# Attention and a softplus feed-forward in one kernel: a new task order for the first chunk, new engines for some tasks, and the mask's load written later

## The chip, the core and the metric

The kernel runs on one core of a Trainium2 chip. The metric is the device time of one execution in microseconds (us). Before the change it is 913.67 us, the median of three runs (913.51 to 913.8).

## The reference

For 8 batches and 8 heads of 576 tokens and 64 channels, attention is computed with a mask: the first four heads see the last 32 keys, the other four see earlier keys at a distance that is a multiple of 32. All sums are in float32.

```
scores = scale * q @ k^T;  scores = where(mask, scores, -1e9)
attn = exp(scores - max);  attn = attn / (sum + 1e-9)
x = (attn @ v) as [4608 tokens, 512]
h = x @ w_in                      # [512, 2048]
g = max(h, 0) + log1p(exp(-|h|))  # softplus
out = g @ w_out                   # [2048, 512]
```

## The kernel before

The 4608 tokens go through the feed-forward in 9 chunks of 512. Each chunk has 16 blocks f of 128 hidden channels. A block is `hidden` (F: 12 matmuls of 128x512 into `ph`), softplus (A, Ae, Al on ScalarE; u, Gh, Gl, which split the result into a high and a low part), and `output` (O: 12 matmuls into four banks `py`). Each product is made of three: high by high, high by the weight's low part, low by high. So x and the weights are split too: x into x_h and x_l (tasks H and L), a weight block into `w_i` or `w_o`.

The weights come as raw 64-bit words. A block is loaded (wi, wo; 512 KB), then `a` on ScalarE, `B`, `d` and `c` on VectorE, then `h` (the high part, a cast) and `l` (the low part, a subtraction) on the engine that three lists name. All 32 blocks are prepared once, in the first chunk, and stay.

Attention works on pairs of heads: pair n has q, k and v loads (q, k, v), the layout of q for its two heads (D), the scores in a long and a short part (S0, S1, which end with a product that adds the mask), the maxima X, then for some parts a subtraction Y, one exponential E and sums Z, for others x and an exponential for each column; then r, R, M (normalisation), the transposes T with their copies C, the products with v (V), and H and L. Digits name the pair and then the part or half: X00 is the maximum of pair 0's long part, L21 the x_l of pair 2's second half. The first chunk of the feed-forward needs pairs 0 to 3. Its first block is cut in two: Fa0 (9 matmuls) needs pairs 0 to 2, F0 also pair 3.

The order of the first chunk is the text table `FIRST` (line 36), one word for each task. A loop near the end calls them in that order, and inside that call each engine's queue gets its instructions in the order written. The lists `ON_POOL`, `ON_VECTOR` and `ON_SCALAR` (from line 61) name tasks that are not on their usual engine. What comes after the first chunk is placed by the class `Plan`, which the change does not touch. Instructions ahead of the table, such as the mask's load and the identity, are not bound to the order in which they are written.

Loads are issued by SP in the table's order; the mask's load is issued by ScalarE. TensorE starts with eight products of no use to the result ("idle", task W).

Of the kernel before, what the change touches and what calls it, by code (L numbers as in the profile page):

```python
# [33 lines left out]


FIRST = """
W q0 k0 D01 D00 S00 S01 X00 Y00 q1 D10 X01 D11 x01 E00 Z00 k1 S11 X11 E01 r0 R0 M0 q2 D21 S10
T00 wi0 D20 Y11 X10 x10 ai0 Bi0 T01 di0 k2 E11 S21 Z11 S20 E10 ci0 v0 r1 C00 R1 M1 X21 x21 C01 V00
wo2 q3 ao2 Bo2 do2 co2 D30 hi0 D31 wi2 T02 C02 X20 Y20 k3 H00 L00 ai2 Bi2 E20 ho2 Z20 T10 wi1 di2
v1 E21 r2 T11 S31 V01 X31 S30 lo2 x31 R2 wo3 C10 T12 ci2 H01 L01 X30 Y30 ai1 C11 V10 C12 hi2 E31  # L40
wo0 M2 H10 L10 li2 E30 Z30 T20 C20 li0 r3 R3 ao3 Bi1 M3 T21 V11 C21 H11 L11 wi11 ai11 Bi11 di1 T22
T32 C32 di11 v2 wi3 V20 C22 H20 ci1 ci11 hi11 L20 T31 ai3 Bi3 v3 hi1 li1 C31 T30 C30 li11 wo1 wi4
V21 H21 L21 V31 di3 wo6 ao1 Bo1 ao0 ci3 V30 H31 L31 H30 L30 Fa0 hi3 li3 do1 Bo0 co1 do0 Bo3 q4 D4
wi12 co0 F0 A0 Ae0 ho1 k5 Al0 u0 lo1 Fa1 k4 S40 ai4 wi6 X40 Bi4 x40 ho0 lo0 wi5 Gh0 ai5 wi7 Bi5 F1
A1 Gl0 ai7 Ae1 Al1 E40 do3 co3 di4 u1 Gh1 ho3 lo3 F2 A2 Ae2 Bi7 ci4 di5 O0 q5 wi10 wo5 ao5 Al2 Gl1
wi8 S41 D5 X41 ci5 x41 E41 u2 Gh2 hi5 di7 li5 F3 hi4 A3 Bo5 do5 ci7 Ae3 Al3 r4 R4 li4 co5 O1 M4
S50 X50 x50 hi7 u3 wo12 v4 F5 F4 ho5 Gl2 lo5 Gh3 Gl3 P4 E50 S51 ai6 ai8 Bi8 di8 X51 O2 wo4 ao4 Bi6
wo7 x51 di6 ci6 hi6 A5 Ae5 Al5 u5 li7 Bo4 q6 A4 E51 r5 k6 D6 V40 ci8 do4 O3 H40 L40 S60 co4 R5
wi13 Ae4 ai10 Bi10 Al4 V41 H41 li6 wi9 M5 u4 Gh4 Gl4 X60 Gh5 ho4 x60 L41 P5 F7 F6 hi8 wo15 lo4 Gl5
li8 di10 v5 O4 k7 E60 ao6 Bo6 A7 ai13 S61 A6 Ae6 V50 O5 Al6 ci10 hi10 do6 co6 u6 wo11 wo8 q7 li10  # L50
F10 Ae7 Al7 X61 ho6 ai9 u7 x61 ao7 Bo7 do7 Bi13 di13 Bi9 Gh7 Gl7 ci13 H50 L50 wo14 lo6 di9 ci9 Gh6
Gl6 F8 D7 E61 r6 S70 co7 A10 Ae10 ao8 Al10 Bo8 do8 R6 hi9 A8 wi15 u10 V51 li9 X70 x70 O6 Ae8 Al8
co8 wo9 u8 M6 H51 L51 wi14 P6 ho8 lo8 ai12 Gh8 ho7 lo7 Gl8 F11 hi13 li13 Bi12 Gh10 Gl10 wo10 ao9
Bo9 F9 O7 E70 S71 ai15 Bi15 do9 X71 co9 v6 ao10 Bo10 A9 Ae9 Al9 x71 do10 V60 H60 L60 u9 ho9 A11 q8
lo9 Ae11 Al11 u11 O8 di15 ci15 Gh11 Gh9 Gl9 di12 V61 H61 ao11 Bo11 wo13 F13 hi15 li15 E71 r7 R7 O9
co10 ho10 A13 ci12 hi12 ao13 Ae13 Al13 k8 v7 Gl11 L61 lo10 do11 F15 ao12 O10 M7 co11 li12 ho11
lo11 u13 Gh13 P7 A15 Ae15 Gl13 ai14 Bi14 di14 ci14 F12 hi14 Al15 u15 O11 q9 A12 Ae12 Al12 u12 Bo12
D8 Gh12 V70 Qa0 li14 F14 do12 co12 ho12 Gl12 lo12 O12 Bo13 do13 A14 co13 ho13 lo13 H70 L70 V71
ao14 Bo14 do14 Ae14 co14 Al14 u14 ho14 lo14 O13 H71 L71 Q1 Gh14 v8 Gl14 O14 ao15 Bo15 do15 co15
Gh15 Gl15 ho15 lo15 QA1 Qu1 Qh1 Ql1 Q0 QA0 O15 y1 Ob15 y2 y3 Qu0 Qh0 y0 Ql0 k9  # L60
"""
# [904 lines left out]
```

## Time and profile before

| | before |
|---|---|
| median of three runs | 913.67 us |
| the profiled execution | 914.04 us |
| its span | 912.0 us |
| TensorE busy | 900.4 us, 99% |
| VectorE busy | 601.9 us, 66% |
| ScalarE busy | 446.3 us, 49% |
| GpSimd busy | 60.1 us, 7% |
| granted TensorE clock | 0.999 |

The span is the time from the first to the last instruction; the execution's time has 2.04 us around it. In the profile PE is TensorE, PEld its loading of weights, DVE VectorE, ACT ScalarE, POOL GpSimd, SP the engine that issues most loads. L328 is line 328: a helper's line can serve many tasks, L256 for instance every copy.

### The profile page before, as it was taken

How to read it: one execution, taken by the hardware profiler on the slowest of the kernel's cores; microseconds unless marked ns; L12 is line 12 of the kernel's file. 1: busy time of each engine (PE TensorE's matmuls, PEld its weight loads, DVE VectorE, ACT ScalarE, POOL GpSimd, SP SyncE). 2: the span in 40 equal slices, each digit the busy share in tenths (PEclk: the TensorE clock that was granted, in tenths of full speed). 3: DMA queues.
4: the chain of work that ended last, by engine and by line, in shares of the span. 5: the costliest groups of instructions: out<-in, count | busy, mean ns of one | idle time of the engine just before them, and what ended most of it. 6: DMA issues, size and time to landing. Idle time of an engine off the chain costs nothing.

```text
span 912.0 us, 14487 instructions
## 1 busy us (share of the span) xinstructions
PE 900.4 (99%) x5700; PEld 725.3 (80%) x5700; DVE 601.9 (66%) x1308; ACT 446.3 (49%) x795; POOL 60.1 (7%) x77
## 2 busy tenths in 40 slices
PE   8899999999999999999999999999999999999998
PEld 5677778888888888888888888888888888888886
DVE  7999997877767667766766676776776333333332
ACT  7898855445444444444544444445443333333332
POOL 4343540000000000000000000000000000000000
PEclk9999999999999999999999999999999999999999
DMA  9927212122211112111211121111200010001001
GB/s 339 349 102 246 81 30 73 43 57 67 70 39 43 43 44 89 32 42 43 89 44 43 43 78 27 42 43 43 89 18 17 1 46 1 1 1 47 0 1 47
DMA packets 49939, 58.27 MB, mean 64 GB/s; under 512 B 3152, under 2 KB 35024, under 8 KB 49872
## 3 DMA queue, kind: packets, MB, share of 16 engines
q1 hardware_dynamic: 49728, 57.16, 19.5%
q8 instruction: 45, 0.74, 0.3%
q10 hardware_dynamic: 144, 0.20, 0.1%
q14 instruction: 22, 0.18, 0.1%
HBM read 47.91 MB, written 9.44 MB: 63 GB/s over the span
## 4 chain that ended last, share of the span: by engine, by line
PE 90%; DVE 6%; ACT 1%; DMA 1%; issue 1%; POOL 0%; SPq 0%; ACTq 0%; DVEq 0%; POOLq 0%
PE py L647 42%; PE ph L607 41%; PE ps L328 3%; PE pv L484 2%; PE po L484 1%; DVE pt L432 1%; PE po L328 1%; DVE u L628 1%; DMA kT<-in_qk_dram 1%; DVE a_o L561 1%; DVE a_i L561 0%; ACT prob L374 0%; DMA raw_q<-in_qk_dram 0%; DVE a_o L578 0%; DVE a_i L578 0%
## 5 line engine op out<-in xcount | busy, mean ns | idle before, releaser
L647 PE MATMUL py<-w_o,gh 128*128 128x512 f32 x1152 | 365.7, 398 | 0.0
L607 PE MATMUL ph<-x_h,w_i 128*128 128x512 f32 x1152 | 358.8, 392 | 0.4 <-DVE u L628 0.4
L619 ACT ACTIVATE u<-ph 128x512 f32<-128x512 f32 x144 | 86.3, 600 | 409.0 <-PE ph L607 409.0
L647 PEld LDWEIGHTS py<-w_o,gh 128*128 128x128 f32 x1152 | 214.4, 188 | 51.8 <-POOL w_o L593 0.9
L607 PEld LDWEIGHTS ph<-x_h,w_i 128*128 128x128 f32 x1152 | 215.8, 188 | 48.9 <-DVE u L628 0.9
L647 PE MATMUL py<-w_o,gl 128*128 128x512 f32 x576 | 227.1, 394 | 0.0
L607 PE MATMUL ph<-x_l,w_i 128*128 128x512 f32 x576 | 225.9, 392 | 0.0
L628 DVE SCALAR_TENSOR_TENSOR u<-ph,u 128x512 f32<-128x512 f32 x144 | 98.9, 688 | 181.0 <-ACT u L624 179.2
L432 DVE STREAM_TRANSPOSE pt<-prob 32x192 f32<-32x192 f32 x448 | 137.1, 314 | 6.4
L647 PEld LDWEIGHTS py<-w_o,gl 128*128 128x128 f32 x576 | 108.6, 189 | 25.7
L607 PEld LDWEIGHTS ph<-x_l,w_i 128*128 128x128 f32 x576 | 108.1, 188 | 25.3
L640 DVE TENSOR_TENSOR gl<-u,gh 128x512 fp32r<-128x512 f32 x138 | 96.1, 697 | 11.2 <-ACT gh L256 0.3
L622 ACT ACTIVATE u<-u 128x512 f32<-128x512 f32 x144 | 91.0, 632 | 4.5
L624 ACT ACTIVATE u<-u 128x512 f32<-128x512 f32 x144 | 90.8, 631 | 4.4
L256 ACT COPY qT<-prob 64x576 f32<-64x576 f32 x56 | 70.6, 1260 | 0.3
L256 DVE CAST gh<-u 128x512 fp32r<-128x512 f32 x130 | 55.4, 426 | 10.6 <-PE py L647 0.5
L391 DVE TENSOR_TENSOR prob<-ps,mask_b 128x384 f32<-128x384 f32 x24 | 13.4, 558 | 53.6 <-PE ps L328 53.6
L328 PEld LDWEIGHTS ps<-kT,qT 128*64 128x64 f32 x720 | 23.6, 137 | 11.7 <-issue 8.8
L328 PE MATMUL ps<-kT,qT 128*64 128x64 f32 x720 | 28.0, 226 | 0.3 <-ACT qT L256 0.3
L484 PE MATMUL pv<-pt,v_in 128*64 128x96 f32 x396 | 22.2, 248 | 0.0
L422 DVE TENSOR_TENSOR prob<-prob,st 128x576 f32<-128x576 f32 x28 | 21.2, 758 | 0.9
L391 DVE TENSOR_TENSOR prob<-po,mask_b 128x192 f32<-128x192 f32 x24 | 8.6, 358 | 19.3 <-ACT x_h L522 19.3
(89 smaller groups left out, 516.7 us busy)
## 6 DMA issues: line engine op xcount, KB each, us to landing
out_dram<-o SPq DMA_DIRECT2D x36, 256.0 KB, 2.2
v_in<-in_v_dram SPq DMA_DIRECT2D x28, 320.0 KB, 3.7
ri<-in_moe_w_in_dram SPq DMA_DIRECT2D x16, 512.0 KB, 7.2
ro<-in_moe_w_out_dram SPq DMA_DIRECT2D x16, 512.0 KB, 7.7
prob<-in_qk_dram SPq DMA_DIRECT2D x28, 288.0 KB, 2.8
kT<-in_qk_dram SPq DMA_DIRECT2D x28, 288.0 KB, 3.0
v_in<-in_v_dram SPq DMA_DIRECT2D x28, 48.0 KB, 2.8
room<-in_v_dram SPq DMA_DIRECT2D x4, 320.0 KB, 7.2
```

Source lines behind the costliest of these rows:

```text
L256: (engine.copy if engine is nc.scalar else engine.tensor_copy)(dst, src)
L328: nc.tensor.matmul(ps[64 * place : 64 * place + 64, 64 * (x - lo) : 64 * (x - lo) + 64], lhsT=blocks_of(n)[:, c // 32].rearrange("p h l -> ...
L391: nc.vector.tensor_tensor(pv, sv, m, op=ALU.add)
L432: nc.vector.transpose(pt[32 * (i + c) : 32 * (i + c) + 32, h, a : a + hi - lo, 32 * i : 32 * i + 32,], src[:, lo:hi, 32 * c : 32 * c + 32],)
L484: nc.tensor.matmul(po[64 * h : 64 * h + 64, TILE * x : TILE * x + TILE], lhsT=vs[n][:, a, h, :], rhs=pt_of(n, a)[:, h, a % 2], start=True, ...
L607: nc.tensor.matmul(ph, lhsT=w32["i", f][:, half, cc * P : (cc + 1) * P], rhs=x_of(x, cc)[:, t0 : t0 + n], start=(i == 0), stop=(i == 3 * N ...
L619: nc.scalar.activation(us[c, f], phs[c, f], AF.Abs)
L622: nc.scalar.activation(u, u, AF.Exp, scale=-1.0)
L624: nc.scalar.activation(u, u, AF.Ln, bias=1.0)
L628: nc.vector.scalar_tensor_tensor(u, in0=phs.pop((c, f)), scalar=0.0, in1=u, op0=ALU.max, op1=ALU.add)
L640: engine.tensor_tensor(g, us.pop((c, f)), ghs[c, f].bitcast(F32), op=ALU.subtract)
L647: nc.tensor.matmul(py[t], lhsT=g[:, sl], rhs=w32["o", f][:, half], start=(f == 0 and n == 0), stop=(f == NFC - 1 and n == 2),)
```

## The change

The table has the same tasks in another order, the lists name other tasks, and the mask's load is written behind the copy of the identity.

```diff
 FIRST = """
-W q0 k0 D01 D00 S00 S01 X00 Y00 q1 D10 X01 D11 x01 E00 Z00 k1 S11 X11 E01 r0 R0 M0 q2 D21 S10
...
-V21 H21 L21 V31 di3 wo6 ao1 Bo1 ao0 ci3 V30 H31 L31 H30 L30 Fa0 hi3 li3 do1 Bo0 co1 do0 Bo3 q4 D4
...
+W wi2 ai2 Bi2 q0 D00 D01 k0 S01 q1 D11 q2 D20 di2 ci2 S00 D10 X01 k1 X00 Y00 E00 S11 X11 Y11 D21
...
+wo7 ao2 T31 q5 C30 v4 wi8 V21 C31 V31 H21 Bi1 D4 di1 ci1 L21 ho3 V30 H31 Fa0 Bo2 lo3 H30 do2 co2
...
 ON_POOL = """
-D10 D20 D30 ho2 r2 x31 hi11 hi3 x40 ho3 x41 hi5 x50 ho5 hi6 r5 x60 ho6 x61 x71 ho9 ho11 Gh13 hi14
-ho13 ho14
+D21 x01 D31 x10 hi2 x21 x31 ho3 hi1 hi7 ho0 x41 x50 ho5 ho4 hi9 x70 Gh11 hi14 ho14 ho15
...
 ON_VECTOR = """
-D00 M0 M1 lo2 C12 M3 li1 li3 lo0 Gl0 lo3 Gl1 li5 li4 li7 li6 li10 Gl7 lo6 Gl6 Gl10 Gl9 li15 Gl11
-lo10 M7 Gh12 li14 Gl12 Gl14 Gh15 Gl15
+D01 D10 M0 M2 M3 li5 li4 lo3 li1 lo2 Gh0 Gl0 lo0 Gh1 lo1 li10 Gl3 lo4 M5 Gl5 Gl6 li12 Gl9 li15
+lo10 Gl13 M7 Gh15 lo12 lo13 Gl14
...
 ON_SCALAR = """
-y1 y3
+y3
...
     mask_b = const.tile([P, 12 * 64], BF16, name="mask_b")
-    nc.scalar.dma_start(mask_b, masks)
...
     nc.scalar.copy(ident, ident_b)
+    nc.scalar.dma_start(mask_b, masks)
```

How the head of ScalarE's queue stands in the built program, before: raw_q are loaded q, early_h laid-out q.

```order
L161 ACT_TABLE_LOAD
L163 DMA mask_b<-in_masks_dram 128x768
L208 CAST room_113<-ident_b 128x128
L256 COPY early_h_91<-raw_q_153 64x32x18
L256 COPY early_h_93<-raw_q_181 64x32x18
L356 ACTIVATE prob_104<-prob_104 128x384
```

And now, where ri is a raw weight block (line numbers are one less, but for the mask's load):

```order
L160 ACT_TABLE_LOAD
L207 DMA mask_b<-in_masks_dram 128x768
L206 CAST room_112<-ident_b 128x128
L547 ACTIVATE a_i_155<-ri_153 128x512
L255 COPY early_h_90<-raw_q_158 64x18x32
L255 COPY early_h_92<-raw_q_170 64x32x18
L255 COPY early_h_94<-raw_q_173 64x18x32
```

The mask's load has kept its place; the step `a` of a weight block stands ahead of the first layout.

TensorE's queue right behind the idle products, before: py are the banks that hold the first scores, early_l holds k.

```order
L328 MATMUL py_106<-early_l_92,early_h_91 64x64 x12
L336 LDWEIGHTS ident_b
L336 MATMUL py_106<-mask_b,ident_b 128x384
L328 MATMUL py_107<-early_l_92,early_h_91 64x64 x6
L336 LDWEIGHTS ident_b
L336 MATMUL py_107<-mask_b,ident_b 128x192
```

And now:

```order
L327 MATMUL py_106<-early_l_91,early_h_90 64x64 x6
L335 LDWEIGHTS ident_b
L335 MATMUL py_106<-mask_b,ident_b 128x192
L327 MATMUL py_105<-early_l_91,early_h_90 64x64 x12
L335 LDWEIGHTS ident_b
L335 MATMUL py_105<-mask_b,ident_b 128x384
```

Pair 0's short part (6 products) now comes ahead of its long part (12).

VectorE's queue from its first copy of q, before: the reduction from a py into st is a maximum X.

```order
L256 COPY early_h_91<-raw_q_153 64x18x32
L364 TENSOR_REDUCE st_178<-py_106 128x6
L351 TENSOR_TENSOR prob_104<-py_106,st_178 128x384
L364 TENSOR_REDUCE st_178<-py_107 128x3
L368 TENSOR_SCALAR st_178<-st_178 128x3
L360 TENSOR_REDUCE st_178<-prob_104 128x6
```

And now:

```order
L551 TENSOR_SCALAR a_i_155<-a_i_155 128x512
L255 COPY early_h_90<-raw_q_158 64x32x18
L560 SCALAR_TENSOR_TENSOR a_i_155<-ri_153,a_i_155 128x512
L577 SCALAR_TENSOR_TENSOR a_i_155<-ri_153,a_i_155 128x512
L255 COPY early_h_92<-raw_q_170 64x18x32
L363 TENSOR_REDUCE st_192<-py_106 128x3
L363 TENSOR_REDUCE st_192<-py_105 128x6
L350 TENSOR_TENSOR prob_103<-py_105,st_192 128x384
```

Three steps of a weight block, a second copy of q and the short maximum have come ahead of X00 (the reduction of size 128x6).

## Rows read from the trace of the kernel before

**Rows 1.** Busy time by stretch: engines, granted clock, DMA share, GB/s.
```profile
0.00:7.54 7.54, 5.62 (x35) 2.65 (x37) 3.16 (x7) 3.93 (x4) 6.65 (x24) 1.00 0.76 245
7.54:35.38 27.84, 22.80 (x524) 16.65 (x524) 26.77 (x56) 22.14 (x65) 10.23 (x11) 1.00 1.01 355
35.38:148.00 112.62, 111.94 (x670) 87.29 (x668) 105.51 (x217) 89.07 (x203) 43.17 (x43) 1.00 0.39 134
```
**Rows 2.** TensorE's waits, whole span: us in total, times, longest.
```profile
PE ph L607 <- DVE u L628: 0.4, 1, 0.4
PE ps L328 <- ACT qT L256: 0.3, 1, 0.3
```
**Rows 3.** TensorE's timeline at Fa0: start, duration, [idle before].
```profile
34.73 0.72 PE L484 MATMUL pv<-early_l,room 128*64 128x96 f32 x12 [1.48 <-DVE x_l L520]
35.38 0.73 PE L607 MATMUL ph<-x_h,w_i 128*128 128x512 f32 x2
```
**Rows 4.** VectorE's timeline, 4 to 35 us.
```profile
4.26 0.73 DVE L256 COPY early_h<-raw_q 64x576 f32<-64x576 f32 x1 [0.33 <-DMA raw_q<-in_qk_dram]
7.54 0.56 DVE L364 TENSOR_REDUCE st<-py 128x6 f32<-128x384 f32 x1 [2.55 <-PE py L336]
...
14.50 1.49 DVE L578 SCALAR_TENSOR_TENSOR a_i<-ri,a_i 128x512 uint32<-128x512 uint32 x1
...
32.56 1.75 DVE L593 TENSOR_TENSOR w_i<-a_i,w_i 128x512 fp32r<-128x512 f32 x1
34.23 0.45 DVE L520 TENSOR_TENSOR x_l<-pv,x_h 128x288 fp32r<-128x288 f32 x1
```
**Rows 5.** TensorE's timeline at the first scores.
```profile
5.51 1.55 PE L328 MATMUL py<-early_l,early_h 128*64 128x64 f32 x24 [0.74 <-ACT early_h L256]
...
7.43 0.91 PE L328 MATMUL py<-early_l,early_h 128*64 128x64 f32 x12
...
8.54 0.91 PE L328 MATMUL py<-early_l,early_h 128*64 128x64 f32 x12
...
9.57 0.92 PE L328 MATMUL py<-early_l,early_h 128*64 128x64 f32 x24
```
**Rows 6.** ScalarE's timeline: the first layouts of q, and D4.
```profile
4.25 1.16 ACT L256 COPY early_h<-raw_q 64x576 f32<-64x576 f32 x1 [1.87 <-DMA raw_q<-in_qk_dram]
5.86 1.19 ACT L256 COPY early_h<-raw_q 64x576 f32<-64x576 f32 x1 [0.45 <-DMA raw_q<-in_qk_dram]
...
36.07 2.56 ACT L256 COPY qT<-prob 64x576 f32<-64x576 f32 x2
```
**Rows 7.** DMA issues, 0 to 60 us: count, KB each, us to landing.
```profile
prob<-in_qk_dram SPq DMA_DIRECT2D x2, 288.0 KB, 5.7
...
mask_b<-in_masks_dram ACTq DMA_DIRECT2D x1, 192.0 KB, 3.7
```
**Rows 8.** GpSimd's timeline.
```profile
8.70 1.25 POOL L256 COPY early_h<-raw_q 64x576 f32<-64x576 f32 x1 [1.15 <-DMA raw_q<-in_qk_dram]
...
32.43 1.32 POOL L593 TENSOR_TENSOR w_i<-a_i,w_i 128x512 fp32r<-128x512 f32 x1
```
**Rows 9.** VectorE by form, 7.5 to 34.2 us: busy us, mean ns | idle before.
```profile
L561 DVE SCALAR_TENSOR_TENSOR a_i<-ri,a_i 128x512 uint32<-128x512 uint32 x4 | 2.7, 686 | 0.0
...
L364 DVE TENSOR_REDUCE st<-py 128x3 f32<-128x192 f32 x4 | 1.4, 352 | 0.0
...
L368 DVE TENSOR_SCALAR st<-st 128x3 f32<-128x3 f32 x2 | 1.1, 556 | 0.1
L414 DVE TENSOR_SCALAR st<-st 128x9 f32<-128x9 f32 x3 | 0.9, 304 | 0.4 <-ACT prob L374 0.4
...
L578 DVE SCALAR_TENSOR_TENSOR a_o<-ro,a_o 128x512 uint32<-128x512 uint32 x1 | 0.7, 692 | 0.0
...
L256 DVE COPY early_h<-pt 128x384 f32<-128x384 f32 x1 | 0.5, 548 | 0.0
...
L368 DVE TENSOR_SCALAR st<-st 128x6 f32<-128x6 f32 x1 | 0.2, 171 | 0.0
```

More of the change, by code (lines that the diff above doesn't have):

```diff
@@ L36 @@
 FIRST = """
-W q0 k0 D01 D00 S00 S01 X00 Y00 q1 D10 X01 D11 x01 E00 Z00 k1 S11 X11 E01 r0 R0 M0 q2 D21 S10
[L38 to L41, printed above, removed]
@@ L42 @@
-T32 C32 di11 v2 wi3 V20 C22 H20 ci1 ci11 hi11 L20 T31 ai3 Bi3 v3 hi1 li1 C31 T30 C30 li11 wo1 wi4
-V21 H21 L21 V31 di3 wo6 ao1 Bo1 ao0 ci3 V30 H31 L31 H30 L30 Fa0 hi3 li3 do1 Bo0 co1 do0 Bo3 q4 D4
[L44 to L59, printed above, removed]
@@ L60 @@
-Gh15 Gl15 ho15 lo15 QA1 Qu1 Qh1 Ql1 Q0 QA0 O15 y1 Ob15 y2 y3 Qu0 Qh0 y0 Ql0 k9
+W wi2 ai2 Bi2 q0 D00 D01 k0 S01 q1 D11 q2 D20 di2 ci2 S00 D10 X01 k1 X00 Y00 E00 S11 X11 Y11 D21
+S10 x01 q3 E01 D31 k2 S20 Z00 E11 X10 r0 wi0 x10 ai0 S21 R0 M0 D30 Bi0 di0 wi3 ai3 X21 hi2 Z11 wi4
+v0 T00 Bi3 T01 C00 T02 ai4 C01 V00 ci0 k3 S31 di3 E10 S30 X20 li2 Y20 ci3 r1 x21 R1 H00 L00 X31
+C02 V01 M1 T11 E20 Z20 wi5 wo3 Bi4 ai5 Bi5 E21 di4 di5 H01 v3 r2 L01 x31 C11 hi0 T10 C10 wo2 R2 M2
+T12 ci5 hi3 E31 X30 Y30 li3 ci4 v1 V10 C12 H10 L10 li0 E30 Z30 T20 C20 hi4 wo0 wi1 T21 C21 wo12 r3
@@ new lines @@
+R3 M3 hi5 li5 k4 V11 H11 L11 v2 ao3 Bo3 do3 ai1 T22 q4 T32 C32 wi7 V20 C22 li4 co3 T30 H20 L20 wo1
+wo7 ao2 T31 q5 C30 v4 wi8 V21 C31 V31 H21 Bi1 D4 di1 ci1 L21 ho3 V30 H31 Fa0 Bo2 lo3 H30 do2 co2
+ao0 ho2 L31 hi1 ai7 L30 li1 lo2 F0 A0 wo4 Ae0 Bi7 S40 X40 Al0 x40 di7 ci7 hi7 Fa1 F1 u0 E40 Bo0
+S41 Gh0 ao1 Bo1 F4 wi11 wi13 A1 Ae1 Al1 wo5 ao5 do0 k6 co0 ho0 X41 D5 x41 u1 F2 wi6 Gl0 Bo5 lo0
+do5 O0 do1 A4 Gh1 co1 co5 Ae4 E41 r4 R4 wo13 Gl1 Al4 wi10 u4 ho1 lo1 ai10 Bi10 di10 k5 A2 Ae2 Al2
+M4 S50 X50 x50 li7 Gh4 Gl4 ho5 F3 wi9 ai9 u2 Gh2 E50 P4 Gl2 A3 O1 wo11 q6 ai6 Ae3 lo5 ci10 ao4 Bi9
@@ new lines @@
+F5 di9 Al3 u3 Bo4 O2 A5 hi10 Bi6 Ae5 li10 wo6 wo10 do4 co4 S51 Gh3 Gl3 Al5 V40 H40 L40 ao6 ho4 X51
+x51 wo8 D6 lo4 E51 Bo6 F7 ai8 A7 Ae7 Al7 di6 ci6 hi6 do6 r5 O3 Bi8 co6 di8 ci8 hi8 R5 S60 li6 u5
+Gh5 V41 H41 X60 ci9 ho6 x60 E60 M5 Gl5 u7 lo6 v5 O4 li8 ao7 Gh7 Gl7 F6 L41 A6 hi9 Ae6 k7 P5 Al6 u6
+F10 wo9 ao9 A10 li9 O5 Ae10 Al10 Bo9 do9 co9 ai13 Bi13 di13 S61 Gh6 wi14 X61 x61 ao8 q7 D7 Bo7 Gl6
+k8 do7 co7 ci13 E61 r6 V50 H50 F8 Bo8 do8 L50 hi13 li13 R6 u10 O6 A8 S70 co8 M6 Ae8 Al8 ho7 ho9
+ai11 lo7 X70 lo9 V51 H51 x70 u8 F9 P6 Gh8 wi12 ai12 v6 ho8 Gl8 E70 lo8 A9 Ae9 Al9 F13 ao11 O7 Gh10
@@ new lines @@
+S71 L51 V60 Bi12 Bi11 di12 ci12 di11 ci11 hi12 li12 O8 H60 ao10 L60 u9 Gl10 X71 wi15 ai15 hi11
+Bo10 do10 V61 Gh9 Gl9 Bi15 A13 H61 x71 Ae13 Al13 co10 di15 ci15 ho10 hi15 wo14 E71 u13 F12 A12
+Gh13 Ae12 li11 Al12 L61 O9 li15 F11 ao12 lo10 Bo11 O10 do11 Gl13 ai14 co11 u12 A11 Bi14 di14 r7 R7
+Ae11 ci14 Al11 M7 F15 Gh12 u11 ho11 v7 Qa0 lo11 ao14 Gh11 Gl11 A15 Ae15 O11 Al15 P7 u15 hi14 li14
+V70 Gl12 Bo12 do12 q8 Gh15 co12 H70 L70 ao13 Bo13 ho12 lo12 F14 A14 Ae14 do13 Bo14 do14 V71 O12
+Al14 u14 Gl15 H71 L71 Q1 wo15 ao15 co13 ho13 co14 lo13 O13 Gh14 Bo15 do15 D8 ho14 Gl14 lo14 co15
@@ L61 @@
+ho15 lo15 QA1 Qu1 Qh1 Ql1 Q0 QA0 Qu0 Qh0 Ql0 O14 Ob15 v8 y3 k9 O15 y2 y0 y1 q9
 """
 ON_POOL = """
-D10 D20 D30 ho2 r2 x31 hi11 hi3 x40 ho3 x41 hi5 x50 ho5 hi6 r5 x60 ho6 x61 x71 ho9 ho11 Gh13 hi14
-ho13 ho14
+D21 x01 D31 x10 hi2 x21 x31 ho3 hi1 hi7 ho0 x41 x50 ho5 ho4 hi9 x70 Gh11 hi14 ho14 ho15
 """.split()
 ON_VECTOR = """
-D00 M0 M1 lo2 C12 M3 li1 li3 lo0 Gl0 lo3 Gl1 li5 li4 li7 li6 li10 Gl7 lo6 Gl6 Gl10 Gl9 li15 Gl11
-lo10 M7 Gh12 li14 Gl12 Gl14 Gh15 Gl15
+D01 D10 M0 M2 M3 li5 li4 lo3 li1 lo2 Gh0 Gl0 lo0 Gh1 lo1 li10 Gl3 lo4 M5 Gl5 Gl6 li12 Gl9 li15
```

## The prediction

> **What bounds the kernel now.** I read the page's busy shares first, then the busy time by stretch, TensorE's waits, and last the timelines of single engines over the first 36 us. After the first 36 us TensorE never rests: from 35.38 to 148 us it is busy 111.94 of 112.62 us, and the waits that are left to it there are 0.4 us for a softplus result and 0.3 us for a q layout [rows 1, 2]. Its number of matmuls is the same in both orders. So the time is TensorE's work plus what it idles, and nearly all its idling lies ahead of the first feed-forward block (Fa0), which starts at 35.38 us [rows 3]. What the change can win or lose is mostly where Fa0 lands.
>
> What holds Fa0 back is VectorE. In the stretch from 7.54 to 35.38 us it is busy 26.77 of 27.84 us, TensorE only 22.80 and ScalarE 22.14 [rows 1]. The last wait before Fa0 is TensorE's, for the subtraction that makes x_l of pair 2's second half (L21): it runs at 34.23 us, releases the product V30 at 34.73, and Fa0 follows at 35.38, 1.15 us after L21 began [rows 3, 4]. VectorE itself gets going at 7.54 us, with the first row maxima (X00), which wait 2.55 us for TensorE's scores [rows 4]. From there to L21 it has 53 instructions and takes 34.23 - 7.54 = 26.7 us. Fa0 is therefore X00's start, plus that list, plus 1.15 us.
>
> **The change, part by part.**
>
> *The mask's load.* In the built order it does not move: on ScalarE it stands behind the table load in both kernels, ahead of the identity's copy, and waits for nothing. Cost 0. Had it moved behind that copy, it would have been issued before the first q is used at 4.25 us, and would be needed only by the first mask product, which ends the first scores [rows 5, 6]; it took 3.7 us to land [rows 7], so the price would be at most a few tenths of a microsecond.
>
> *The new head.* SP now sends a weight block (wi2, 512 KB) ahead of q0 (288 KB) and k0. Before, q0 is used at 4.25 us, the third load of that size (q1) at 5.86, the fifth (q2) at 8.70: 0.8 us for each load at first, 1.4 later [rows 6, 8]. 512 KB are 1.78 such loads, so q0 comes at 4.25 + 1.78 x 0.8 = 5.7, and k0 as load 3.78 at 6.5 to 7.0. ScalarE's half of the layout takes 1.16 and ends near 6.9; VectorE's half lies beside it. The first scores start at about 7.0 instead of 5.51 [rows 5, 6].
>
> The second step is their order: the short part S01 now goes ahead of S00, and X00 needs S00. Before, 2.03 us lie between S00's start and X00 (5.51 to 7.54), and S01 with its mask takes 1.11 (7.43 to 8.54). These are slow matmuls: the same 24 take 1.55 us at 5.51 and 0.92 at 9.57, a ratio of 0.6 [rows 4, 5]. At the slow pace X00 comes at 7.0 + 1.11 + 2.03 = 10.14; at the fast one the two parts take 0.6 x 3.14 = 1.9 and it comes at 8.9. The late end, if k0 takes a load's time more, is 11.0. Which pace holds then is not shown by the trace; I take the slow one, since before it still holds at 8.54 (twelve matmuls in 0.91). So X00 is 2.6 us late, with the ends +1.3 and +3.5.
>
> The granted clock reads 1.00, the 2.4 GHz level, in the stretch up to 7.54 us too, while the first scores' matmuls run slower than their twins at 9.57 [rows 1, 5]. The Trainium skill (TensorE: Matmul & The Clock Gate, Part 1: The HAM clock gate) says that the slow clock is the default and activity lifts it. The pause ahead of the first scores grows from 0.74 us to about 2.2, so by that rule S01 and S00 run slow, and the sum is the +2.0 below; at the fast pace it would be +0.7. No run here shows it yet.
>
> In the time until then VectorE prepares wi2 (L552, L561, L578, 0.69 us each at most), lays out two halves of q (0.73 each by the copy it had) and takes X01 (0.35): under 3.9 us that start near 5.5, when wi2 is there, and end before 10.1 [rows 4, 9]. That is real work out of the way, but of a later weight block, not of the list between X00 and L21.
>
> *The list from X00 to L21.* In the new order 51 instructions stand there. Against before it has one L561, one L578 and one L414 more (0.69, 0.69, 0.30), and one copy of transposed probabilities, one short maximum and three L368 fewer (0.55, 0.35, and 2 x 0.56 + 0.17) [rows 9]. By these means that is -0.5 us; with the undisturbed 0.17 for each L368 and L414 it is +0.1. I take 0, with those ends.
>
> *Collisions with GpSimd.* Some VectorE instructions took far longer than their twins while GpSimd was working: L578 1.49 and L593 1.75 instead of the 0.69 of an undisturbed L578 (GpSimd's own L593 ran from 32.43 to 33.75), and two L368 took 0.56 in the mean where a third took 0.17 [rows 4, 8, 9]. These cost 0.80 + 1.06 + 0.78 = 2.6 us. Before, six long GpSimd instructions (two q copies, one normalisation, three weight subtractions) stand in this stretch; the new lists put six of the same kinds there. Which VectorE instruction meets them is not shown. I take no difference; the ends are -2.6 (all gone) and +2.0 (two more).
>
> The Trainium skill (SBUF — State Buffer, SBUF: two separate sides) calls the port pair that VectorE shares with GpSimd "an exclusive lock, not a bandwidth split", held for a whole instruction. The rows agree in the one case: VectorE's L593 ended 0.56 after GpSimd's. By that rule each of the six could hold VectorE up for its whole 1.3 us, 7.8 in all, so the late end of the sum would be +5.2 over before rather than +2.0.
>
> *Everything behind Fa0.* The order of blocks and weights to the end of the first chunk is new too, with three GpSimd instructions fewer and three g_low more on GpSimd. TensorE's work there is the same, and VectorE's, by the counts of the two built orders, by less than 1 us. It costs only where TensorE waits. Before it waits 0.7 us there [rows 2]; reaching every block later, it gives its suppliers more time, so I take 0.6 off. The ends are -0.7 and +1.5. The copies of the results (one moved from ScalarE to VectorE) lie beside TensorE's next block.
>
> *The sum.* 2.6 + 0 + 0 - 0.6 = +2.0 us. The profiled execution took 914.04 us (span 912.0 and 2.04 around it), 0.37 over the median of the runs; 914.04 + 2.0 = 916.0, or 915.7 on the scale of the median 913.67.
>
> **The rivals.**
>
> *The lateness is absorbed.* The fast pace, k0 early and no wait behind Fa0: +1.3 - 0.7 = +0.6, or 914.3. For it: where the pace changes is seen in one execution only. Against it: it was still slow at 8.54 before, with a shorter pause ahead.
>
> *GpSimd's new places cost VectorE nothing* (not slower). VectorE reads scores from PSUM while GpSimd copies; the collisions go: 2.6 - 2.6 - 0.6 = -0.6 on the median, 913.1; at the fast pace too -1.9, or 911.8. It decides from 2.0 us of collisions gone, where the sum is zero. For it: the lists are spread anew, and one small maximum and its scaling leave VectorE. Against it: as many long GpSimd instructions stand in the same stretch, beside the same weight work.
>
> *ScalarE is late with the last x* (slower still). D4, two copies of 2.56 us together [rows 6], stands in the new table ahead of H31 and H30; before it came behind them. Both are needed for F0, which stands right behind Fa0's nine matmuls. If q4, which took 5.7 us to land [rows 7], lands only when L21 runs, F0 waits up to 2.6: +4.6, or 918.3. Against it: ScalarE idles 5.7 of 27.84 us there [rows 1] and should reach D4 early.
>
> **How the numbers follow.** About 0.2% (1.83 us: 911.84 to 915.50) is what a measurement of this kernel can tell from no change. The forecast has 0.45, its own range 914.6 to 916.8, and some 0.11 of it lie inside the bound. The absorbed lateness has 0.25, nearly all of it within. GpSimd has 0.15, of which 0.09 are faster. The late x has 0.15, nearly all slower. Together: faster 0.10, within 0.42, slower 0.48. The range leaves out the ends where several terms fall on one side: 912.4 to 918.6.
>
> **What would show it.** Right: wi2 lands first, S01 starts near 7.0 and X00 near 10.1; L21 and Fa0 2 to 3 us later than 34.23 and 35.38; the stretch from X00 to L21 again close to 26.7; the mask's issue still at 0.75; TensorE without idling from Fa0 to 148 us. Wrong: X00 before 8.9 (the head), a stretch X00 to L21 under 25 (collisions or list), or TensorE idling over 1.5 us between Fa0 and the end of the first chunk (the blocks' new order). If Fa0 is not later than 35.38 and the time still grows, the whole reading of the head is wrong.

## The result, and the profile after

The changed kernel takes 916.40 us (median of 6 runs, 915.91 to 917.76); the kernel before took 913.64 beside it (6 runs, 912.82 to 914.08). The ratio is 1.0033, 95% interval 1.0020 to 1.0046: slower by 2.8 us, where 2.0 were forecast. The profiled execution took 916.61 us, its span is 914.6.

TensorE's timeline of the kernel after (start, duration, what ran, idle time before it) answers to [rows 3, 5]:

```profile
7.20 0.57 PE L327 MATMUL py<-early_l,early_h 128*64 128x64 f32 x12 [2.43 <-ACT early_h L255]
...
7.88 0.99 PE L327 MATMUL py<-early_l,early_h 128*64 128x64 f32 x24
8.81 0.50 PE L335 MATMUL py<-mask_b,ident_b 128*128 128x384 bf16 x1
10.01 0.91 PE L327 MATMUL py<-early_l,early_h 128*64 128x64 f32 x12 [0.70 <-ACT early_h L255]
...
11.12 1.55 PE L327 MATMUL py<-early_l,early_h 128*64 128x64 f32 x24
...
38.31 0.72 PE L606 MATMUL ph<-x_h,w_i 128*128 128x512 f32 x2
```

The short part S01 starts at 7.20 us and S00 at 7.88, both at the fast pace; the mask product that ends S00 runs from 8.81 to 9.31, and from there on the products are slow (S10: 1.55 for 24). Fa0 starts at 38.31, 2.93 us later than before [rows 3].

VectorE's timeline of the kernel after, its starts and its long steps up to L21, answers to [rows 4]:

```profile
5.83 0.51 DVE L551 TENSOR_SCALAR a_i<-a_i 128x512 uint32<-128x512 uint32 x1 [1.91 <-ACT a_i L547]
...
8.39 1.52 DVE L255 COPY early_h<-raw_q 64x576 f32<-64x576 f32 x1
9.84 0.80 DVE L363 TENSOR_REDUCE st<-py 128x3 f32<-128x192 f32 x2
...
13.15 0.56 DVE L363 TENSOR_REDUCE st<-py 128x6 f32<-128x384 f32 x1 [0.70 <-PE py L335]
...
14.06 1.22 DVE L421 TENSOR_TENSOR prob<-prob,st 128x576 f32<-128x576 f32 x1
15.21 1.49 DVE L551 TENSOR_SCALAR a_i<-a_i 128x512 uint32<-128x512 uint32 x1
...
25.94 1.76 DVE L577 SCALAR_TENSOR_TENSOR a_i<-ri,a_i 128x512 uint32<-128x512 uint32 x1
...
37.16 0.45 DVE L519 TENSOR_TENSOR x_l<-pv,x_h 128x288 fp32r<-128x288 f32 x1
```

The row at 9.84 is two maxima, X01 and then X00, which therefore starts near 10.08 (9.84 + 0.80, less the 0.56 that X00 took before). VectorE did not wait there: the scores were ready at 9.31, and it was still in its own queue. From X00 to L21 are 37.16 - 10.08 = 27.1 us.

The long GpSimd steps of the kernel after answer to [rows 8]:

```profile
8.14 1.36 POOL L255 COPY early_h<-raw_q 64x576 f32<-64x576 f32 x1 [2.09 <-DMA raw_q<-in_qk_dram]
...
14.76 1.66 POOL L592 TENSOR_TENSOR w_i<-a_i,w_i 128x512 fp32r<-128x512 f32 x1
...
25.61 3.21 POOL L592 TENSOR_TENSOR w_i<-a_i,w_i 128x512 fp32r<-128x512 f32 x2 [2.10 <-DMA ro<-in_moe_w_out_dram]
```

Each lies beside a long row of VectorE's. The busy time by stretch of the kernel after (length, busy time of PE, PEld, DVE, ACT and POOL with counts, granted clock, DMA share, GB/s) answers to [rows 1]:

```profile
7.20:10.14 2.94, 2.24 (x40) 1.59 (x42) 2.91 (x5) 2.51 (x2) 1.36 (x1) 0.74 1.04 400
10.14:37.16 27.02, 22.56 (x498) 16.56 (x498) 25.63 (x53) 21.09 (x65) 9.77 (x11) 0.90 0.86 300
37.16:38.31 1.15, 0.65 (x12) 0.53 (x13) 1.15 (x4) 1.14 (x2) 0.61 (x1) 1.00 0.93 336
38.31:148.00 109.69, 109.02 (x659) 85.65 (x658) 103.36 (x215) 88.10 (x201) 42.40 (x38) 1.00 0.38 131
```

L21 to Fa0 is 1.15 again. Behind Fa0 TensorE lacks 0.67 us up to 148 us, against 0.68 before [rows 1], and TensorE's waits (us in total, times, longest) name 0.6 of it, for k of pair 5 [rows 2]:

```profile
PE pv L483 <- DVE x_l L519: 4.5, 5, 2.1
...
PE ps L327 <- DMA kT<-in_qk_dram: 0.6, 1, 0.6
```

The span grew by 2.6 and Fa0 came 2.93 later: what is to be explained is the head. The 0.3 us that came back behind it are no more than profiles differ there (next section).

### The profile page after: what moved, and what is told of

Its sections match the earlier page's. It is cut to its first block, busy times and chain, and to the rows that moved or that the text cites. A ratio compares the mean times of both kernels' runs of the same rounds, so it can differ in the third digit from the quotient of the medians.

```text
span 914.6 us, 14491 instructions
## 1 busy us (share of the span) xinstructions
PE 900.8 (98%) x5700; PEld 726.0 (79%) x5700; DVE 603.9 (66%) x1310; ACT 447.8 (49%) x796; POOL 59.3 (6%) x74
## 4 chain that ended last, share of the span: by engine, by line
PE 94%; DVE 3%; DMA 1%; ACT 1%; issue 0%; SPq 0%; DVEq 0%; ACTq 0%
PE py L646 44%; PE ph L606 43%; PE ps L327 3%; PE pv L483 2%; PE po L483 1%; PE po L327 1%; DMA kT<-in_qk_dram 1%; DMA ri<-in_moe_w_in_dram 0%; DVE a_i L577 0%; DVE a_i L560 0%; DVE a_i L551 0%; ACT prob L373 0%; DVE st L363 0%; DVE early_h L255 0%; DVE x_l L519 0%
## 5 line engine op out<-in xcount | busy, mean ns | idle before, releaser
L606 PEld LDWEIGHTS ph<-x_l,w_i 128*128 128x128 f32 x576 | 108.1, 188 | 25.5 <-DVE x_l L519 0.3
```

The costliest lines, as they stand in the source:

```text
L606: nc.tensor.matmul(ph, lhsT=w32["i", f][:, half, cc * P : (cc + 1) * P], rhs=x_of(x, cc)[:, t0 : t0 + n], start=(i == 0), stop=(i == 3 * N ...
```

## The experiments

All were timed beside the kernel before, whose medians in the four sessions lay between 913.31 and 913.41. In the diffs only the words of the table that move are shown, for e2, e7 and e8 at their new place only. "After" is the changed kernel. Its own interval is 1.8 to 4.2 us above the kernel before, and it was timed in another session, so differences of under about 1 us between the medians of after and of its versions are not clear of noise; the profiles, one execution each, show where the time lies. In every profile but four, the stretch from Fa0 to the end of the span is 876.0 to 877.0 us, so Fa0's start is the first number to look at; the four are e1, e7, e9 and e12.

**e2: the load of wi2 alone.**

```diff
-W q0 k0 D01 D00
+W wi2 q0 k0 D01 D00
```

> The kernel before with one word moved: the load of wi2 is issued first, ahead of q0 and k0; all computing on wi2 stays where it was. Theory (the load's price goes through): the first layout of q starts 1.2 to 1.5 us later than 4.25, S00 at 6.7 to 7.0, X00 at 8.7 to 9.1, and Fa0 and the time are 1.2 to 1.5 us later than before. Rival (a late start is absorbed between X00 and Fa0, since later loads and transposes then wait less): X00 is late by the same, Fa0 by less than 0.7, time under +0.6 us.

914.66 us, ratio 1.0014 (1.0006 to 1.0023). ScalarE's first layout, and VectorE's X00 and L21:

```profile
5.87 1.16 ACT L256 COPY early_h<-raw_q 64x576 f32<-64x576 f32 x1 [3.49 <-DMA raw_q<-in_qk_dram]
```

```profile
9.15 0.56 DVE L364 TENSOR_REDUCE st<-py 128x6 f32<-128x384 f32 x1 [2.58 <-PE py L336]
...
35.20 0.44 DVE L520 TENSOR_TENSOR x_l<-pv,x_h 128x288 fp32r<-128x288 f32 x1
```

q came 1.62 us later than in [rows 6], X00 1.61, L21 0.97. The list was 0.6 shorter because the collisions fell differently: one small step of VectorE took 0.17 instead of 0.94. The median rose by 1.25. So the load's price goes through in the time, as the prediction had it, though Fa0 came only 0.96 later, less than the theory's 1.2 to 1.5.

**e8: the load and the steps of wi2 in front, scores in the old order.**

```diff
-W q0 k0 D01 D00 S00
+W wi2 ai2 Bi2 q0 k0 D01 D00 di2 ci2 S00
```

> The kernel before with the load of wi2 in front as in e2 and also its steps ai2, Bi2, di2, ci2, as in after; the scores keep the old order, the long part first. Theory (VectorE's list from X00 to Fa0 sets the time): X00 starts at 9.1 as in e2, but three steps of 0.42 to 0.69, 1.7 us together, have gone from the list behind it, so Fa0 comes 0.6 to 1.0 us earlier than before's 35.38 and the time is 912.4 to 912.9. Rival (the prediction's reading: a late start goes through and the steps put ahead of X00 are no gain): the time is that of e2, 1.0 to 1.5 us above before. Rival (collisions fall differently): any value between, with a VectorE step of 1.3 us or more that was short in before.

914.14 us, ratio 1.0012 (1.0003 to 1.0021). X00 started at 9.22 and L21 at 34.68: the stretch is 25.5 us against 26.05 in e2. So the steps that run while the scores are awaited do come off the list, but of their 1.7 us only about 0.5 arrived at L21 and in the medians (a difference that the intervals of e2 and e8 do not separate); 0.76 went into new waits of VectorE for ScalarE (0.53 for an x_h, 0.23 for an exponential), the rest I cannot name. The result lies between the first theory and the first rival.

**e3: the long part first.**

```diff
-k0 S01 q1 D11 q2 D20 di2 ci2 S00 D10
+k0 S00 q1 D11 q2 D20 di2 ci2 S01 D10
```

> The kernel after with S00 and S01 exchanged, so that the long part is multiplied first. The prediction's step (the short part ahead of the long one is what X00 waits for): X00 starts 0.6 to 1.1 us earlier than 10.1 and the time falls by 0.6 to 1.1 us from after. Rival (X00 waits for VectorE's own queue: the steps of wi2, two layouts and X01 stand ahead of it, and the scores have been ready since 9.3 us): X00 and Fa0 stay within 0.2 us of after, the time too.

916.70 us (915.49 to 918.49), ratio 1.0039 (1.0027 to 1.0052): no gain over after. In this profile VectorE's D10 began at 8.39, just ahead of GpSimd's D21 at 8.46; this time D10 took 0.69 and GpSimd's copy 1.67. The pair of maxima started at 9.28, waiting only 0.20 for TensorE, and X00 came at 9.5 and L21 0.66 earlier than in after, but the time did not follow. D10 was 0.83 shorter, which by itself is more than the 0.5 at X00, so the prediction's 1.1 us for putting the short part ahead are not there.

**e4: no collision ahead of X00.**

```diff
-D20 di2 ci2 S00 D10 X01 k1 X00 Y00 E00 S11 X11 Y11 D21
+D20 D21 di2 ci2 S00 D10 X01 k1 X00 Y00 E00 S11 X11 Y11
 ON_POOL = """
-D21 x01 D31
+x01 D31
```

> The kernel after with the layout of q2's second half (D21) on ScalarE, right behind D20, instead of on GpSimd. In after GpSimd's copy ran from 8.14 to 9.50 and VectorE's layout D10 took 1.52 us beside it instead of 0.65. Theory (VectorE's queue ahead of X00, stretched by that collision, sets X00): D10 takes about 0.7, X00 starts 0.6 to 0.9 us earlier than 10.1, Fa0 follows by as much, time 0.5 to 0.9 us below after. Rival (X00 waits for the scores or the time is lost elsewhere): D10 is short but Fa0 and the time stay within 0.2 us of after; or ScalarE's extra 1.2 us delays the first exponential and S20, and the time is 0.3 to 1.0 us above after.

916.02 us (915.36 to 917.69), ratio 1.0034 (1.0022 to 1.0045). D10 took 0.68, and X00 still started at 10.0, now waiting for the scores. TensorE and VectorE in this profile:

```profile
7.98 1.55 PE L327 MATMUL py<-early_l,early_h 128*64 128x64 f32 x24
...
55.00 0.92 PE L327 MATMUL ps<-kT,qT 128*64 128x64 f32 x24 [1.60 <-DMA kT<-in_qk_dram]
```

```profile
10.01 0.56 DVE L363 TENSOR_REDUCE st<-py 128x6 f32<-128x384 f32 x1 [0.67 <-PE py L335]
```

Here the slow products began 0.8 us earlier than in the profile of after, in S00. So two limits stand within 0.2 us of each other at X00, VectorE's queue and slow scores, and taking one away leaves the other. The list was a microsecond shorter (26.04), mostly because after's step of 1.76 us took 0.69 here and the wait of 0.70 was gone, so Fa0 came at 37.20. S50 then waited 1.6 us for k5, which landed at 55.0 as in after: of 1.1 us at Fa0, 0.5 reached the span and 0.4 the median.

**e7: k5 ahead of k6, on top of e4.**

```diff
-F1 u0 E40 Bo0 S41 Gh0 ao1 Bo1 F4 wi11 wi13
+F1 u0 E40 Bo0 S41 Gh0 ao1 Bo1 F4 k5 wi11 wi13
```

> e4 with one word moved: the load k5 stands ahead of wi11 and so ahead of k6, whose issue waits until S41 has read its buffer. In e4 Fa0 came 1.1 us earlier than in after, but the time fell by only 0.4: S50 waited 1.6 us (in after 0.6) for k5, which landed at 55.0 us in both. Theory (that load gives the gain back): the wait is gone, Fa0 as in e4 near 37.2, and the time is 1.3 to 1.7 us below e4, 914.3 to 914.8. Rival (the loads are one full queue, and another one is late instead, a weight block for F2 or F3): the wait for k5 goes and another of 0.8 us or more comes; time less than 0.6 below e4.

917.94 us (916.80 to 919.51), ratio 1.0049 (1.0036 to 1.0062): by the medians slower than e4 by 1.9, with intervals that overlap. The wait for k5 went, and TensorE's waits show others in its place:

```profile
PE ps L327 <- ACT prob L373: 1.2, 2, 0.7
...
PE py L646 <- DVE w_o L592: 0.6, 1, 0.6
```

These are 1.2 us in S41 and S50 and 0.6 for a weight's low part. This execution also had slow scores from the start (S01 0.91, X00 at 10.28, Fa0 at 38.29), which is no effect of k5. From Fa0 to the end of the span it is 877.7 us against 876.9 in e4, so 0.8 lies behind Fa0, where k5 can be the cause. That the loads are one full queue fits; the rest of the 1.9 stays open.

**e5: the pause ahead of the scores filled.**

```diff
-    first["W"] = lambda: dummies(8)
+    first["W"] = lambda: dummies(12)
```

> The kernel after with 12 idle products ahead of the first scores instead of 8, to fill the pause of 2.4 us (4.77 to 7.20) in which TensorE waits for q. In after the granted clock falls to 0.50 at 8.7 us, behind that pause, and comes back at 15.3; S10 takes 1.55 instead of 0.92 and VectorE waits 0.70 for it. Theory (the fall follows the pause): the granted clock stays 1.00 from 7 to 16 us, the scores run in 0.92 and 0.57, and the time falls by 0.3 to 1.2 us. Rival (the fall has nothing to do with the pause): a stretch at 0.50 is there as in after, and the time stays within 0.2 us. Third (it costs): the added products are still running when q is laid out, S01 starts after 7.4 and the time grows by 0.2 us or more.

915.31 us (9 runs, 914.64 to 916.51), ratio 1.0024 (1.0015 to 1.0034); 7 of the 9 runs lie below the lowest of after's. Busy time by stretch, after (first fence) and e5 (second):

```profile
7.20:8.50 1.30, 1.30 (x33) 1.14 (x35) 1.27 (x3) 1.16 (x1) 0.36 (x1) 1.00 1.03 402
8.50:15.50 7.00, 6.30 (x88) 4.63 (x82) 6.16 (x12) 5.28 (x13) 3.98 (x6) 0.51 1.09 387
```

```profile
7.20:10.14 2.94, 2.60 (x55) 2.00 (x57) 2.87 (x6) 2.31 (x2) 1.46 (x2) 1.00 1.04 400
10.14:16.00 5.86, 5.52 (x142) 4.04 (x141) 5.72 (x12) 5.78 (x17) 3.91 (x6) 1.00 1.10 378
28.00:34.00 6.00, 5.95 (x119) 4.25 (x122) 5.83 (x13) 5.21 (x12) 0.61 (x1) 0.72 0.55 178
```

In after TensorE has the 1.2 GHz level from 8.6 to 15.4 us; in e5 it keeps 2.4 GHz past 16, all the first scores are fast, VectorE waits for none of them, and Fa0 comes at 36.60. A fall came here too, but at 29.6 to 33 us. Not all of the gain is the clock's. VectorE's D10, GpSimd's D21 and TensorE's Fa0 in e5:

```profile
8.26 0.68 DVE L255 COPY early_h<-raw_q 64x576 f32<-64x576 f32 x1
```

```profile
8.59 1.40 POOL L255 COPY early_h<-raw_q 64x576 f32<-64x576 f32 x1 [2.25 <-DMA raw_q<-in_qk_dram]
```

```profile
36.60 0.72 PE L606 MATMUL ph<-x_h,w_i 128*128 128x512 f32 x2
```

D10 was not stretched, since q2 landed later than in after and GpSimd began behind it. That is 0.84 of the 1.71 us by which Fa0 came earlier, and e3 had it without any change to the pause; the wait for S10 that went is 0.70. The median fell by 1.1, or by 0.8 when each version is taken against the kernel before of its own session. How much of that is the pause, and how much q2's landing, is not separated.

**e10: hi2 and li2 earlier on GpSimd.**

```diff
-S10 x01 q3 E01 D31 k2 ... X21 hi2 Z11 ... X20 li2 Y20
+S10 x01 q3 E01 D31 hi2 li2 k2 ... X21 Z11 ... X20 Y20
 ON_POOL = """
-D21 x01 D31 x10 hi2
+D21 x01 D31 hi2
```

> The kernel after with hi2 and li2 directly behind D31 in GpSimd's queue, ahead of x10, and x10 on VectorE (0.17 us). In after li2 ran on GpSimd from 14.76 to 16.42, and beside it VectorE's normalisation M0 took 1.22 us instead of 0.76 and the step Bi0 1.49 instead of 0.42: 1.5 us together. Theory (the collisions are part of the list that sets Fa0): both are short, the stretch from X00 to L21 shrinks from 27.0 to 25.6 to 26.2, and the time falls by 0.7 to 1.4 us from after, 915.0 to 915.7. Rival (the collision only moves to another VectorE step): another step grows by 0.7 us or more, and the time stays within 0.4 us of after. Rival (VectorE's list has slack elsewhere): short steps, but new waits of VectorE of 0.7 us or more ahead of L21.

916.35 us (915.90 to 916.60), ratio 1.0035 (1.0022 to 1.0047). The two steps were as short as expected, and Fa0 came 1.26 us earlier than in after. VectorE, then TensorE:

```profile
14.23 0.76 DVE L421 TENSOR_TENSOR prob<-prob,st 128x576 f32<-128x576 f32 x1
14.91 0.42 DVE L551 TENSOR_SCALAR a_i<-a_i 128x512 uint32<-128x512 uint32 x1
```

```profile
37.05 0.73 PE L606 MATMUL ph<-x_h,w_i 128*128 128x512 f32 x2
...
44.47 0.57 PE L327 MATMUL ps<-kT,qT 128*64 128x64 f32 x12 [0.47 <-ACT prob L373]
...
54.42 0.92 PE L327 MATMUL ps<-kT,qT 128*64 128x64 f32 x24 [0.86 <-DMA kT<-in_qk_dram]
```

The span fell by 0.6 and the median by 0.05. No theory named this: the collision is real, the list sets Fa0, and half of the gain ends in waits behind Fa0 (0.47 and 0.86, where after had 0.6 in all). Whether the other half is there in the time is not clear of noise.

**e11: e5 and e10 together.** The diffs are those two.

> e10 and e5 together: the kernel after with 12 idle products, hi2 and li2 behind D31, x10 on VectorE. e5 was 1.1 us below after. Theory (the two causes are separate terms of Fa0's time): the gains add, time 1.8 to 2.5 us below after, 913.9 to 914.6, and Fa0 near 35.5. Rival (they overlap, since in a faster start x10 or S20 reaches the collision at another time): no more than the larger one, 915.0 to 915.4.

915.84 us (914.60 to 917.75), ratio 1.0030 (1.0018 to 1.0041). By the medians no more than e5 alone, so the gains do not add; but the runs spread over 3 us, and the profiled one is the fastest, with a span 2.1 below after's. This version too has fast first scores and an unstretched D10, and its median is only 0.6 below after's, so the 1.1 of e5 is not firm either. In the profile Fa0 came at 36.46, and M0 took 1.67 beside GpSimd's moved li2: in the faster start the collision is back.

**e6 and e9: the collision of li1 with li11, in the kernel before.** In [rows 4, 8] VectorE's last weight step ahead of L21 takes 1.75 us beside GpSimd's L593.

```diff
-C30 li11 wo1 ... L30 Fa0 hi3 li3
+C30 wo1 ... L30 Fa0 li11 hi3 li3
```

> The kernel before with one word moved: li11, GpSimd's subtraction for weight block 11, from ahead of Fa0 to right behind it. In before it ran from 32.43 to 33.75 on GpSimd while VectorE's li1, the last weight step ahead of L21, took 1.75 us (32.56) instead of 0.69. Theory (that length is a collision with GpSimd, and VectorE's list sets Fa0): li1 takes 0.7, L21 and Fa0 come 0.9 to 1.1 us earlier, and the time falls by 0.7 to 1.1 us. Rival (VectorE is not what sets Fa0, or the collision moves to another step): Fa0 stays within 0.3 us and the time too. Rival (behind Fa0 the gain is given back): Fa0 earlier by 1, time less than 0.3 below.

913.28 us (11 runs), ratio 0.9998 (0.9989 to 1.0006). The word moved, but no GpSimd task stands between its old and its new place, so every engine's queue is as before: a second measurement of the kernel before. li1 again took 1.75. Yet its profile differs from the first one, which is useful. TensorE in it:

```profile
5.47 0.92 PE L328 MATMUL py<-early_l,early_h 128*64 128x64 f32 x24 [0.70 <-ACT early_h L256]
...
34.19 0.73 PE L607 MATMUL ph<-x_h,w_i 128*128 128x512 f32 x2
```

S00 ran in 0.92 instead of 1.55, X00 came at 6.69 instead of 7.54, Fa0 at 34.19 instead of 35.38, and the span is 910.6 instead of 912.0. e9 puts the word behind hi3:

```diff
-C30 li11 wo1 ... L30 Fa0 hi3 li3
+C30 wo1 ... L30 Fa0 hi3 li11 li3
```

> The kernel before with li11 behind hi3. e6 moved the word only behind Fa0, where no other GpSimd task stood between its old and its new place, so GpSimd's queue was the same as in before, and so were the collision and the time. Here GpSimd first makes hi3, which waits for H30 (36.3 us in before), so its subtraction no longer lies beside VectorE's li1. Theory (collision, and VectorE's list sets Fa0): li1 takes 0.7 instead of 1.75, L21 and Fa0 come 1.0 us earlier against X00, and the time falls by 0.7 to 1.1 us from before, 912.3 to 912.7. Rival (the length of li1 is not from GpSimd): li1 stays over 1.2 us, time within 0.2 us. Rival (given back, since li11's result or its buffer is late for something behind Fa0): Fa0 earlier, time less than 0.3 below.

915.91 us (915.33 to 916.51), ratio 1.0030 (1.0019 to 1.0042): slower by 2.6. VectorE, ScalarE and TensorE:

```profile
32.16 0.68 DVE L593 TENSOR_TENSOR w_i<-a_i,w_i 128x512 fp32r<-128x512 f32 x1
33.00 0.46 DVE L520 TENSOR_TENSOR x_l<-pv,x_h 128x288 fp32r<-128x288 f32 x1 [0.15 <-ACT x_h L522]
...
37.97 0.82 DVE L520 TENSOR_TENSOR x_l<-pv,x_h 128x288 fp32r<-128x288 f32 x2 [2.98 <-ACT x_h L522]
```

```profile
36.99 0.66 ACT L548 ACTIVATE a_o<-ro 128x512 f32<-128x512 f32 x1 [3.46 <-POOL w_i L593]
37.55 0.68 ACT L522 CAST x_h<-pv 128x288 fp32r<-128x288 f32 x2
```

```profile
34.16 0.73 PE L607 MATMUL ph<-x_h,w_i 128*128 128x512 f32 x2
...
38.29 0.73 PE L607 MATMUL ph<-x_h,w_i 128*128 128x512 f32 x2 [1.80 <-ACT x_h L522]
```

li1 was short, L21 and Fa0 (34.16) came 1.2 us earlier than in the profile of before, and all of it and more was lost: the weight steps share four temporary tiles, li11 held one until 37.0, ScalarE's ao0 waited 3.46 us for it, and H31 and H30, which F0 needs, stood behind ao0 in ScalarE's queue.

**e12: L21 ahead of li1, in the kernel before.**

```diff
-v3 hi1 li1 C31 ... V21 H21 L21 V31
+v3 hi1 C31 ... V21 H21 L21 li1 V31
```

> The kernel before with li1 directly behind L21 on VectorE instead of ahead of it. In e9 the stretched li1 went from L21's way and Fa0 came 1.2 us earlier, but li11, now late on GpSimd, held its temporary tile; of these there are four, so ScalarE's step ao0 waited for it until 37.0 us, with H31 and H30 queued behind it, F0 waited 1.8 us and the time rose by 2.6. Here GpSimd's queue stays as it was, and li1 still ends near 34.3, where ScalarE's ao1 takes its tile over. Theory (Fa0's time sets the end as long as H30 is not late): L21 at 33.0 to 33.3 where X00 is at 7.5, Fa0 0.9 to 1.2 us earlier against X00, no new wait at F0, time 0.6 to 1.2 us below before, 912.1 to 912.7. Rival (the tile ring or ScalarE is a second bound just behind): ao1 or H31 comes later than in before by 0.3 us or more, F0 waits 0.5 to 1.5, and the time is within 0.4 us of before.

913.33 us (11 runs, 912.64 to 914.43), ratio 1.0004 (0.9995 to 1.0013): no change. Its profile has the fast start of e6, with X00 at 6.70 and a span of 910.6 in both. The first softplus result u0 on VectorE, e6 (first fence) and e12 (second), and TensorE's wait for it in e12:

```profile
39.80 0.69 DVE L628 SCALAR_TENSOR_TENSOR u<-ph,u 128x512 f32<-128x512 f32 x1 [0.23 <-ACT u L624]
```

```profile
39.61 0.69 DVE L628 SCALAR_TENSOR_TENSOR u<-ph,u 128x512 f32<-128x512 f32 x1 [0.33 <-ACT u L624]
```

```profile
32.98 0.74 PE L607 MATMUL ph<-x_h,w_i 128*128 128x512 f32 x2
...
40.36 0.74 PE L607 MATMUL ph<-x_h,w_i 128*128 128x512 f32 x2 [0.43 <-DVE u L628]
```

Fa0 came 1.21 us earlier than in e6, u0 only 0.19. ScalarE's ao1 takes over li1's tile, and H31, H30, D4 and the logarithm's steps follow it there without a gap; that chain moved by 0.19, and TensorE waited out the rest. ScalarE is the second bound, and right behind the first: an earlier Fa0 alone, with li1 and ScalarE's chain behind it where they were, is worth nothing. Where the whole head came earlier, as in e6's profile against the first one of before, the span fell with Fa0.

**e1: the new head with the old order behind it.** Tasks up to H31 in the new order and places, the others, Fa0 among them, in the old. On TensorE Fa0 still follows V30.

```diff
 FIRST = """
+W wi2 ai2 Bi2 q0 D00 D01 k0 S01 ... L21 ho3 V30 H31 Bo2 do2 co2 ho2 lo2 wi11 ai11
+Bi11 ... ao0 L31 H30 L30 Fa0 do1 Bo0 co1 do0 wi12 co0 F0
...
```

> The new table up to Fa0, with its engines, and behind Fa0 the remaining tasks in the old order with the old engines. Theory (the head): the whole difference is that Fa0 lands 2.9 us later, and the new order behind it costs and gains nothing. Then Fa0 stands near 38.3 us here too and the time is 2.4 to 3.0 us above before. Rival (the new order behind Fa0 has a cost of its own, hidden in the sum): the old order gives back part of the lateness, and the time is only 0.5 to 1.8 us above before. If the new order behind Fa0 is the better one, the time is more than 3.2 us above before.

927.06 us, ratio 1.0147 (1.0133 to 1.0161). Fa0 came at 38.28, as expected, but the time tells nothing on the order behind it: what was left of the old order began with weight blocks that the old head had loaded early and the new one had not. ScalarE and TensorE:

```profile
46.52 0.66 ACT L548 ACTIVATE a_i<-ri 128x512 f32<-128x512 f32 x1 [6.58 <-DMA ri<-in_moe_w_in_dram]
```

```profile
50.74 1.22 PE L607 MATMUL ph<-x_h,w_i 128*128 128x512 f32 x2 [10.13 <-ACT x_h L522]
```

H30 stood behind those steps, and F0 waited 10.1 us for it. The seam cost far more than either half.

## Why the prediction was right, and where not

The time lies in the range, 0.7 above the forecast and inside the forecast's own range. By its steps:

- *The mask's load.* Right: its issue stands at 0.75 us in both profiles.
- *The load of wi2.* Right: the first layout stands at 5.87 (5.7 foretold) and S01 at 7.20 (7.0); e2 measures the load alone as 1.25 us.
- *The short part ahead, slow.* X00 came at 10.1 as foretold (10.14), but in the profile of after this step failed, and that the number agreed there is in part luck. S01 and S00 ran fast and were ready at 9.31. What X00 waited for was VectorE's own queue of wi2 steps, layouts and X01, which the prediction had under 3.9 us and ending before 10.1: from 5.83 it took 4.3 and ended there, since GpSimd's copy stretched D10 from about 0.69 to 1.52. The foretold slow scores are the other limit, 0.2 us away (e4, 10.01; e7, 10.28). In e1, whose order is the same up to there, the step came as foretold: S01 took 0.91, S00 1.55, and X00 waited 1.01 us for them, until 10.21. So which of the two limits holds differs between executions. Exchanging the parts won nothing (e3).
- *The pace.* The prediction took S01 and S00 as slow behind the pause. For this it drew on the Trainium skill (TensorE: Matmul & The Clock Gate, Part 1: The HAM clock gate), by which the slow clock is the default and activity lifts it. After's profile shows both fast, e1's both slow, and in after the 1.2 GHz level comes only from 8.6 us on. In all eight profiles with a pause of about 2.4 us some of the first scores took 1.55; in the two with 12 idle products none did. That fits a price of the pause, paid through later products: S10 made VectorE wait 0.70. But of the four profiles with a pause of 0.7 us two have slow first scores and two have none, so two clean starts do not show it alone, and e5 adds products as well as filling the pause.
- *The list from X00 to L21.* 27.1 against 26.7, foretold equal. Collisions: 0.83 ahead of X00, and in the list 0.46 + 1.07 + 1.07 = 2.6 (over 0.76, 0.42 and 0.69), against 0.77 + 0.80 + 0.41 + 1.06 = 3.0 before [rows 4, 9]. The foretold "no difference" holds nearly. VectorE is busy 25.7 us in this stretch against 25.6 before, and idle 1.4 against 1.1; its longest wait is 0.70 for S10 now and was 0.41 for an exponential. The Trainium skill (SBUF — State Buffer, SBUF: two separate sides) calls the port pair that the two engines share an exclusive lock; the 7.8 us that the prediction worked out from it, an estimate, did not come.
- *Behind Fa0.* Foretold 0.6 back because suppliers have more time; measured 0.3, within what profiles differ by. TensorE's idling up to 148 us did not shrink: the waits of before went, and one for k5 came.

The sum was 2.0 and the median rose by 2.76. In the profile the head gives it: X00 2.5 later, the list 0.4 longer, 0.3 back. The experiments do not split it further: e8 has 0.8 with the wi2 group in front, but its scores are slow behind the pause too, and e5 wins 0.8 to 1.1 with two things changed at once. What the prediction did not see is that bringing Fa0 alone forward need not pay: in e12 1.2 us were worth nothing, in e10 half of 1.3 us was lost behind it. e9's loss is the mechanism of the third rival (ScalarE late with the last x), which after itself does not have: no wait for x_h stands in its list. Of the rival that the lateness is absorbed, the fast pace came true in after, but e2 shows that the load's lateness reaches the time; the one that GpSimd's places cost nothing fell with the rows above. No version here beats the kernel before; the nearest, e12, is the same within its interval.

## What to carry to other kernels

When one engine's last wait sets the start of a long busy stretch, look up what is next behind it before pricing a gain: in e12 ScalarE's chain stood 0.2 us behind, so a gain of 1.2 us at that one place did not pass, while in e2 a delay of the whole head did. Follow the ring of temporaries as well as the queues, since a step made late on an idle engine can hold the tile that a busy one waits for. And a load put in front is paid by what needs the loads behind it: here 1.25 us, of which the work that it enabled in the gap gave back about 0.5 (e2, e8). Last, an experiment's profile is one execution: e5 changed the pause, and a load that landed 0.45 us later changed as much beside it.
